# Attention, a ReLU MoE and a routed MoE on one core: the mask added by TensorE, global rows copied once, and the hand-over to the routed experts re-ordered

## The chip, the core and the metric

The kernel runs on one of the cores of a Trainium2 chip. Five engines each take their instructions in order: TensorE (PE; its weight loads are listed as PEld), VectorE (DVE), ScalarE (ACT), GpSimd (POOL) and SyncE (SP, which here issues most of the DMAs). They meet by semaphores only. The metric is the device time of one execution in microseconds, as a median of several runs; the profile is of one further execution.

## What is computed

```python
def reference(...):
    # 1. attention, 4 batches x 8 heads, 512 local + 32 global rows, head_dim 64
    out_g = softmax(scale * q_g @ [k_g, k_l]^T) @ [v_g, v_l]
    s_ll  = where(|i - j| <= 32, scale * q_l @ k_l^T, -1e9)
    out_l = softmax([scale * q_l @ k_g^T, s_ll]) @ [v_g, v_l]
    x = concat([out_g, out_l]) as 2176 tokens x 512
    # 2. MoE 1: two dense layers, 512 -> 2048 -> 512, leaky ReLU 0.01
    x = leaky(x @ w_in) @ w_out
    # 3. MoE 2: each token goes to one of 8 experts (argmax of cosine / tau)
    e = argmax(logits);  out = gate * (relu(x @ w1[e]) @ w2[e])   # 512 -> 1024 -> 512
```

The weights of MoE 1 arrive as 64-bit floats and are converted on the chip.

## The kernel before

**Three stages overlap.** The front (slots 0 to 20) does attention alone, while ACT, DVE and POOL convert w_in and w_out (`conv`: two ACT casts of the raw words, three DVE operations on bits, one ACT cast and one POOL subtraction for each of 32 pieces). Then the loop over `steps` runs MoE 1 (`L1`, `L2`) on PE with the rest of the attention between its matmuls. Last come 22 or more blocks of MoE 2, 128 tokens of one expert each.

**Attention.** `QK(n, 0)` and `QK(n, 1)` transpose the keys and queries of a pair of heads into `kT` and `qz`; `gnp` holds the transposed global rows, from which `kg` (global keys) and `gz` (global queries, padded with zeros so that one head stands in each half) are copied. `S(p)` multiplies, and DVE takes each 128x224 piece of scores, adds the mask, scales, writes it to SBUF and keeps the minimum (L211); ACT takes the exponential of it (L217); DVE divides (L223). `TR` transposes the probabilities, `AV` multiplies by the values. `GS`, `GT`, `GA` do the same for global rows. PSUM slots are shared by tag, two to a tag: `bank` says which tag a tile takes (S, H, Y or T), and a tile whose name isn't in it takes T.

**MoE 2.** Blocks alternate between two lanes: even blocks s use the expert weights in w1a and w2a, odd ones those in w1b and w2b (`load_w`, a conditional DMA that is skipped if the lane already holds that expert). Matmuls are done in three passes of fp32r, so the weights have to be split into a high and a low part: ACT casts 128x1024 (L849) and DVE subtracts (L850), 8 pieces a block. `M1(s, j)` is one half of the first layer, `HT(s, j)` transposes the hidden half (`tp`, then ACT cast and DVE subtraction `ht`), `M2(s, j)` is the second layer, `X2(s)` transposes the gathered tokens (`xgp`, `xgT`). The hidden half `hs` is cut at zero by ACT for j = 0 and by DVE for j = 1.

**The hand-over.** The last three token tiles leave MoE 1 only when blocks 0 and 1 could begin. Their routing is woven into the blocks by the table `due`: `Q1` (transpose `x2p` and logits `lp`), `Q2` (argmax, 11 small DVE operations), `Q3` (ranks `rp` and counts `cp` by matmul), `Q4` (positions, then three scatters of ids by POOL and six stores of rows by SP), `late_plan` (the plan for blocks 6 and later, 32 small DVE operations). `first` is the list of the weight pieces of block 0, which are split during the last steps of MoE 1. `half` is a pool of 8 buffers that holds first the weights of MoE 1 and then w1b, w2b and the split weights.

**What sets the order.** PE's order is that of the code everywhere. DVE's and SP's are that of the code in blocks 0 to 3. Elsewhere a scheduler orders DVE, ACT, POOL and SP when the kernel is built; an engine never overtakes within its order at run time.

Of the kernel before, what the change touches and what calls it, by code (L numbers as in the profile page):

```python
# [11 lines left out]
I32 = mybir.dt.int32  # L12
# [8 lines left out]
NEG = -8.0e9  # L21
# [3 lines left out]
def kernel(  # L25
# [114 lines left out]
    gzs = [att.tile([P, 2, SG], F32, name=f"gz{i}") for i in range(2)]  # L140
    for t in gzs:
        nc.vector.memset(t[D:P, 0], 0.0)
        nc.vector.memset(t[0:D, 1], 0.0)
# [7 lines left out]
    bank = {"sp0": "S", "sp1": "H", "sg1": "S"}  # L151
# [6 lines left out]
    def QK(n, j):  # L158
        qn, kn, gn = natural[n]
        if j == 1:  # L160
# [4 lines left out]
            nc.scalar.copy(qz, qv)  # L165
# [93 lines left out]
    def GS(n):  # L259
        sg1 = ps.tile([P, SL], F32, tag=bank_of("sg1"), name="sg1")  # L260
        sg2 = ps.tile([P, SG], F32, tag=bank_of("sg2"), name="sg2")
        for j in range(4):
            o = slice(SG * j, SG * j + SG)
            kT, gz = qkT[n - 1 + j // 2]
            lq = gz[:, j % 2, :]
            nc.tensor.matmul(sg1[o, :], lq, kT[:, :, 0:P], start=True, stop=True, tile_position=(0, SG * j))
            nc.tensor.matmul(
                sg2[o, :], lq, kT[:, NC - 1, P:P + SG], start=True, stop=True, tile_position=(0, SG * j)
            )
# [59 lines left out]
    def conv_load(i):  # L329
# [226 lines left out]
    def Q1(q):  # L556
# [36 lines left out]
    def Q3():  # L593

        ob = lt_["ob3"]
        rp = ps.tile([P, NL, E], F32, tag="T", name="rp")
# [7 lines left out]
        cp = ps.tile([1, E], F32, tag="T", name="cp")  # L604
# [121 lines left out]
    def make_plan(early):  # L726
# [33 lines left out]
        else:  # L760
            V.tensor_tensor(out=nb, in0=nb, in1=taken, op=ALU.subtract)
        V.tensor_tensor(out=pre, in0=lt, in1=nb.unsqueeze(1).to_broadcast([1, E, E]), op=ALU.mult)
# [4 lines left out]
        else:  # L767
# [9 lines left out]
            posf = pos.rearrange("o l i -> o (l i)")  # L777
        shp = [1, n, E]
# [8 lines left out]
        V.tensor_reduce(out=ex, in_=a2, axis=AX.X, op=ALU.add)  # L787
        if early:
# [18 lines left out]

        m = n // NLANE
# [80 lines left out]
    def M1(s, j):  # L889
# [9 lines left out]
        if j == 0:  # L899
# [311 lines left out]
```

## Time and profile before

| what | value |
|---|---|
| time, median of 3 runs (range) | 933.41 us (931.83 to 934.14) |
| the profiled execution, its own time | 931.04 us |
| its span, first to last instruction | 929.1 us |
| PE, PEld busy | 93 %, 78 % |
| DVE, ACT, POOL busy | 69 %, 60 %, 19 % |
| mean granted TensorE clock | 0.963 |

Busy shares are means over stages that have different limits, so the profile is read stage by stage: the table of stretches gives for each engine how much of a stretch it was busy, the timeline gives single instructions with the idle time ahead of them in brackets and what ended it, and the granted clock is 1.00 at 2.4 GHz and 0.50 at 1.2 GHz.

### The profile page before, as it was taken

Reading aid. Unit: us, or ns where it says so; the run is one execution under the profiler, and the core shown is the slowest. Engines: PE = TensorE matmul, PEld = TensorE weight load, DVE = VectorE, ACT = ScalarE, POOL = GpSimd, SP = SyncE. Lnnn points to the kernel's source line nnn. Section 1 sums busy time; section 2 is a strip of 40 time slices with the busy share of each in tenths; the row PEclk is TensorE's granted clock in tenths of the full one; section 3 lists DMA queues with packets and bytes.
Section 4 is the critical chain, followed back from the end, with each engine's and each line's share of the span. In section 5 each row is a group of like instructions: output and inputs, shape, how many; then the busy total and the mean of one; then the engine's idle time right before and its main releaser. Section 6 shows DMA issues by size and latency. Waiting matters only on the chain.

```text
span 929.1 us, 15882 instructions
## 1 busy us (share of the span) xinstructions
PE 863.6 (93%) x5578; PEld 727.1 (78%) x5578; DVE 639.2 (69%) x1557; ACT 561.6 (60%) x1206; POOL 173.5 (19%) x220
## 2 busy tenths in 40 slices
PE   3766799999999999999999999997899999999997
PEld 2555587888888888888888988986687888888885
DVE  6998888444664654554544435556989989999996
ACT  5877876544544644445433232364687888888885
POOL 3423433000210110010000000120233222231311
PEclk9776799999999999999999999997999999999999
DMA  8875562120122121110000000554315118829550
GB/s 215 197 215 149 146 189 69 33 45 17 29 61 44 25 57 29 44 30 3 13 12 1 24 1 24 193 187 73 24 58 215 35 46 328 276 78 384 191 202 26
DMA packets 104995, 92.68 MB, mean 100 GB/s; under 512 B 73735, under 2 KB 82055, under 8 KB 104914
## 3 DMA queue, kind: packets, MB, share of 16 engines
q1 hardware_dynamic: 97618, 77.47, 27.7%
q0 software_dynamic: 4224, 10.78, 4.2%
q10 hardware_dynamic: 3072, 3.41, 1.2%
q8 instruction: 45, 0.74, 0.4%
q14 instruction: 36, 0.29, 0.1%
HBM read 140.03 MB, written 11.63 MB: 163 GB/s over the span
## 4 chain that ended last, share of the span: by engine, by line
PE 73%; DVE 9%; issue 6%; DMA 6%; ACT 5%; POOL 1%; SPq 1%; POOLq 0%; ACTq 0%; DVEq 0%
PE hps L669 20%; PE hp L895 10%; PE yp L923 9%; PE yp L691 7%; PE yp L693 6%; PE yp L692 6%; PE av L247 3%; PE pp L233 2%; PE sp L199 2%; PE tp L909 2%; DMA qn<-in_q_l_dram 1%; DMA ids<-idl 1%; ACT pr L217 1%; PE lp L499 1%; DVE pr L223 1%
## 5 line engine op out<-in xcount | busy, mean ns | idle before, releaser
L676 ACT COPY gf<-hps 128x256 f32<-128x256 f32 (+1 forms) x144 | 50.2, 360 | 175.2 <-PE hps L669 168.4
L677 DVE SCALAR_TENSOR_TENSOR gf<-gf 128x256 f32<-128x256 f32 (+1 forms) x144 | 60.7, 429 | 129.3 <-ACT gf L676 127.7
L895 PE MATMUL hp<-w1s,xgT 128*128 128x512 f32 x528 | 139.1, 413 | 0.0
L923 PE MATMUL yp<-w2s,ht 128*128 128x512 f32 x528 | 130.9, 396 | 1.0 <-DVEq L1175 1.0
L923 PEld LDWEIGHTS yp<-w2s,ht 128*128 128x128 f32 x528 | 98.8, 188 | 25.7 <-DVEq L1175 1.4
L895 PEld LDWEIGHTS hp<-w1s,xgT 128*128 128x128 f32 x528 | 100.0, 196 | 21.4
L691 PE MATMUL yp<-woh,g 128*128 128x512 f32 x272 | 114.8, 422 | 0.0
L693 PE MATMUL yp<-woh,g 128*128 128x512 f32 x272 | 107.7, 396 | 0.0
L692 PE MATMUL yp<-wol,g 128*128 128x512 f32 x272 | 107.7, 396 | 0.0
L680 DVE TENSOR_TENSOR g<-gf,g 128x256 fp32r<-128x256 f32 (+1 forms) x144 | 57.7, 409 | 39.3 <-ACT g L679 35.0
L669 PE MATMUL hps<-xs,wih 128*128 128x256 f32 x448 | 75.7, 291 | 5.7 <-ACT gf L676 4.2
L679 ACT CAST g<-gf 128x256 fp32r<-128x256 f32 (+1 forms) x144 | 55.3, 395 | 36.1 <-DVE gf L677 36.1
L669 PEld LDWEIGHTS hps<-xs,wih 128*128 128x128 f32 x448 | 65.0, 189 | 12.5 <-ACT gf L676 4.9
L669 PE MATMUL hps<-xs,wil 128*128 128x256 f32 x448 | 71.3, 281 | 0.0
L669 PE MATMUL hps<-xl,wih 128*128 128x256 f32 x448 | 71.2, 280 | 0.0
L217 ACT ACTIVATE pr<-pr,nm 128x224 f32<-128x224 f32 x128 | 60.6, 475 | 2.7 <-DVE nm L211 1.8
L693 PEld LDWEIGHTS yp<-woh,g 128*128 128x128 f32 x272 | 51.2, 188 | 12.7 <-DVE g L680 0.2
L669 PEld LDWEIGHTS hps<-xs,wil 128*128 128x128 f32 x448 | 60.9, 189 | 0.0
L669 PEld LDWEIGHTS hps<-xl,wih 128*128 128x128 f32 x448 | 60.9, 189 | 0.0
L691 PEld LDWEIGHTS yp<-woh,g 128*128 128x128 f32 x272 | 51.3, 189 | 11.7 <-issue 4.5
L850 DVE TENSOR_TENSOR w2s<-w2a,w2s 128x1024 fp32r<-128x1024 f32 x48 | 56.7, 1218 | 2.8 <-ACT w2s L849 2.6
L850 DVE TENSOR_TENSOR w1s<-w1a,w1s 128x1024 fp32r<-128x1024 f32 x48 | 56.5, 1217 | 1.8 <-ACT w1s L849 1.7
(257 smaller groups left out, 1705.1 us busy)
## 6 DMA issues: line engine op xcount, KB each, us to landing
w1a<-in_moe_w_dram SPq DMA_DIRECT2D x12, 2048.0 KB
w2a<-in_moe_w_dram SPq DMA_DIRECT2D x12, 2048.0 KB
w1b<-in_moe_w_dram SPq DMA_DIRECT2D x12, 2048.0 KB
w2b<-in_moe_w_dram SPq DMA_DIRECT2D x12, 2048.0 KB
raw<-in_moe_w_in_dram SPq DMA_DIRECT2D x13, 512.0 KB
raw<-in_moe_w_out_dram SPq DMA_DIRECT2D x13, 512.0 KB
x2d<-x SPq DMA_DIRECT2D x16, 256.5 KB
kn<-in_k_l_dram SPq DMA_DIRECT2D x31, 128.0 KB
```

Of the source, the lines that this page charges most:

```text
L217: nc.scalar.activation(out=pr, in_=pr, func=AF.Exp, bias=nm[:, j:j + 1], scale=-1.0, accum_out=sm[:, j:j + 1],)
L669: nc.tensor.matmul(hps, ws[a][:, k], xs[c][k], start=(a + c + k == 0), stop=((a, c) == (1, 0) and k == KM - 1))
L676: nc.scalar.copy(gf, hps[:, cs])
L677: nc.vector.scalar_tensor_tensor(out=gf, in0=gf, scalar=0.01, in1=gf, op0=ALU.mult, op1=ALU.max)
L679: nc.scalar.copy(g[:, 0], gf)
L680: nc.vector.tensor_tensor(out=g[:, 1], in0=gf, in1=g[:, 0].bitcast(F32), op=ALU.subtract)
L691: nc.tensor.matmul(yp, g[:, 0], hi, start=(f == 0), stop=False)
L692: nc.tensor.matmul(yp, g[:, 0], lo, start=False, stop=False)
L693: nc.tensor.matmul(yp, g[:, 1], hi, start=False, stop=(f == KF - 1))
L850: nc.vector.tensor_tensor(out=w[:, 1, c], in0=src[:, c], in1=w[:, 0, c].bitcast(F32), op=ALU.subtract)
L895: nc.tensor.matmul(hp_, xT[:, a, k, :], w[:, c, k, :], start=(a + c + k == 0), stop=(c == 1 and k == KM - 1))
L923: nc.tensor.matmul(yp, ht[:, a, f, :], w[:, c, f, :], start=(j + a + c + f == 0), stop=(j == c == 1 and f == 3))
```

## The change

1. **Mask by PE in the front.** While the front's bank table is in force, a bf16 identity times the bf16 mask starts each score tile (one 128x448 matmul for each of the two heads), and the score matmuls add to it. DVE takes the maximum straight from PSUM, two reductions of 2x224 instead of four masked passes, and ACT's exponential reads PSUM instead of SBUF. The factor 0.125 goes into the copy of `qz`. After the front the old form stays.
2. **Global rows copied once.** `gz` holds keys and queries side by side, in one copy from `gnp` instead of three; `GS` uses the 64 partitions of each head instead of zero padding. The two border copies of `kT` go from DVE to ACT. In the front `kp` takes tag H and `gnp` takes tag S instead of T.
3. **First raw loads** of the conversion are issued by SP, behind the first q, instead of by ACT.
4. **Second lane loaded in MoE 1.** `load_w(1)` stands at step 10 of MoE 1's last round instead of behind it; `first` holds only the two halves of w1 of block 0, and its w2 follows behind the last step.
5. **Late routing.** Logits, ranks and counts share one tile on tag Y; logits become a step of their own (`Q1L`); Q2 to Q4 come later, and `late_plan` is cut in five pieces between places of blocks 1 and 2.
6. **`hs`** is cut at zero by ACT for both halves of blocks 0 to 4.

```diff
+    ALONE = dict(sp0="S", sp1="H", sg1="S", pp="Y", av="T", gp="Y", gq="T", ga="T", qp="T", kp="H", gnp="S")
-        nc.vector.tensor_copy(kT[:, 1:NC, 0:SG], kp[:, 0:NC - 1, P - SG:P])
-        nc.vector.tensor_copy(kT[:, 0:NC - 1, WIN - SG:WIN], kp[:, 1:NC, 0:SG])
+        nc.scalar.copy(kT[:, 1:NC, 0:SG], kp[:, 0:NC - 1, P - SG:P])
+        nc.scalar.copy(kT[:, 0:NC - 1, WIN - SG:WIN], kp[:, 1:NC, 0:SG])
...
-        nc.vector.tensor_copy(kg, gp[:, 0:SG])
-        for h in range(2):
-            r = slice(64 * h, 64 * h + 64)
-            nc.vector.tensor_copy(gz[r, h, :], gp[r, SG:2 * SG])
+        nc.vector.tensor_copy(gz.rearrange("p a s -> p (a s)"), gp)
...
+        for h in range(2 if pe_mask else 0):
+            nc.tensor.matmul(sps[h], identb, mask[:, kind(c0):kind(c0) + 2, :], start=True, stop=False)
...
+            if pe_mask:
+                nc.vector.tensor_reduce(
+                    out=nm[:, 2 * h:2 * h + 2], in_=sps[h], axis=AX.X, op=ALU.max, negate=True
+                )
+                continue
...
-            (nc.scalar if i < 6 else nc.sync).dma_start(t, src.bitcast(I32))
+            (nc.scalar if 2 <= i < 6 else nc.sync).dma_start(t, src.bitcast(I32))
...
+            rt["bank"] = ps.tile([P, 2 * NL + 1, E], F32, tag="Y", name="lr")
...
-        if j == 0:
+        if j == 0 or s < 5:
             nc.scalar.activation(out=hs, in_=hp_, func=AF.Relu)
...
+                load_w(1)
+                first = pieces_w1(0, 0) + pieces_w1(0, 1)
...
+    for piece in pieces_w2(0, 0) + pieces_w2(0, 1):
+        tc.keep_in_program_order(piece())
...
-        (0, "a"): [(Q1, (0,)), (Q1, (1,))], (0, "b"): [(Q1, (2,))], (0, "c"): [(Q2, ())],
-        (0, "d"): [(Q3, ())], (0, "e"): [(Q4, ())], (1, "a"): [(late_plan, ())],
+        (0, "a"): [(Q1, (0,)), (Q1, (1,))], (0, "b"): [(Q1L, (0,)), (Q1L, (1,)), (Q1, (2,))], (0, "d"): [(Q1L, (2,))],
+        (0, "e"): [(Q2, ())], (1, "a"): [(Q3, ())], (1, "c"): [(Q4, ())], (1, "e"): [(late_plan, ())],
+        (1, "f"): [(late_plan, ())], (2, "a"): [(late_plan, ())], (2, "d"): [(late_plan, ())], (2, "e"): [(late_plan, ())],
```

**Where instructions move.** On PE, at the hand-over, before: the first M1 of block 0 (`hp_7324`), the routing of the late tiles, the second M1 of block 0 (`hp_7362`), and the first M1 of block 1 (`hp_7500`) behind ranks and counts.

```order
L895 MATMUL hp_7324<-w1s,xgT 128x512 x12
L560 MATMUL x2p<-ident,x_7310 128x128 x4
L566 MATMUL lp<-enT,x2T 128x8 x4
L560 MATMUL x2p<-ident,x_7314 128x128 x4
L566 MATMUL lp<-enT,x2T 128x8 x4
L895 MATMUL hp_7362<-w1s,xgT 128x512 x12
L560 MATMUL x2p<-ident,x_7318 128x128 x4
L566 MATMUL lp<-enT,x2T 128x8 x4
L909 MATMUL tp<-ident,hs 128x128 x4
L881 MATMUL xgp<-ident,xg 128x128 x4
```

The same place on PE after the change; `lr` is the shared tile, `hp_7317` the second M1 of block 0, `hp_7435` the first M1 of block 1.

```order
L910 MATMUL hp_7288<-w1s,xgT 128x512 x12
L565 MATMUL x2p<-ident,x_7264 128x128 x4
L565 MATMUL x2p<-ident,x_7268 128x128 x4
L910 MATMUL hp_7317<-w1s,xgT 128x512 x12
L576 MATMUL lr<-enT,x2T 128x8 x8
L565 MATMUL x2p<-ident,x_7272 128x128 x4
L924 MATMUL tp<-ident,hs 128x128 x4
L896 MATMUL xgp<-ident,xg 128x128 x4
L576 MATMUL lr<-enT,x2T 128x8 x4
L924 MATMUL tp<-ident,hs 128x128 x4
L910 MATMUL hp_7435<-w1s,xgT 128x512 x12
```

The logits of the first two late tiles went behind the second M1 of block 0, and ranks and counts behind the first M1 of block 1.

On DVE at the same place, before, from the copies of the late tiles on: the hidden half of `hp_7362`, the argmax (first and last row of 11), then block 1's pieces of w1b.

```order
L562 COPY x2T<-x2p 128x512 x2
L902 TENSOR_SCALAR hs<-hp_7362 128x512
L562 COPY x2T<-x2p 128x512
L580 TENSOR_SCALAR sl_7304<-sl_7304,tau_sb 128x3
...
L590 TENSOR_TENSOR lg_7305<-lg_7305,sl_7304 128x24
L850 TENSOR_TENSOR w1s<-w1b,w1s 128x1024 x2
L912 TENSOR_TENSOR ht<-tp,ht 128x512
L884 TENSOR_TENSOR xgT<-xgp,xgT 128x512
```

DVE after the change, from the same copies to the same argmax.

```order
L567 COPY x2T<-x2p 128x512 x2
L865 TENSOR_TENSOR w2s<-w2a,w2s 128x1024 x3
L567 COPY x2T<-x2p 128x512
L865 TENSOR_TENSOR w2s<-w2a,w2s 128x1024
L865 TENSOR_TENSOR w1s<-w1b,w1s 128x1024 x2
L927 TENSOR_TENSOR ht<-tp,ht 128x512
L899 TENSOR_TENSOR xgT<-xgp,xgT 128x512
L590 TENSOR_SCALAR sl_7258<-sl_7258,tau_sb 128x3
```

Four pieces of w2a and two of w1b now stand ahead of the argmax, and the hidden half is gone from DVE.

On SP at the program's start after the change, the raw loads stand between the first q and the second pair's keys; before, ACT issued them, behind its own k and q.

```order
L88 DMA kn<-in_k_l_dram 128x4x64
L94 DMA gn<-in_k_g_dram 32x4x64
L94 DMA gn<-in_q_g_dram 32x4x64
L88 DMA qn<-in_q_l_dram 128x4x64
L345 DMA raw<-in_moe_w_in_dram 128x4x256
L345 DMA raw<-in_moe_w_out_dram 128x1024
```

Two loads of 512 KB moved from ACT's queue to SP's.

## Rows read from the trace of the kernel before

**Rows 1.** Busy time by stretch: PE, PEld, DVE, ACT, POOL us; PE clock, DMA share, GB/s.

```profile
0.00:106.00 106.00, 66.87 (x519) 50.48 (x520) 89.94 (x261) 80.10 (x205) 39.73 (x67) 0.79 0.74 194
...
150.00:616.00 466.00, 464.86 (x3387) 406.25 (x3383) 241.02 (x885) 210.29 (x619) 42.27 (x71) 1.00 0.14 37
616.00:725.00 109.00, 96.53 (x451) 78.29 (x450) 87.56 (x138) 73.91 (x99) 25.39 (x21) 0.92 0.42 114
```

**Rows 2.** Timeline of PE at the hand-over: start us, us, instruction [idle before <-releaser].

```profile
621.62 2.96 PE L895 MATMUL hp<-w1s,xgT 128*128 128x512 f32 x12
...
661.86 1.12 PE L909 MATMUL tp<-ident,hs 128*128 128x128 f32 x4 [3.83 <-DVE hs L902]
...
689.05 3.08 PE L895 MATMUL hp<-w1s,xgT 128*128 128x512 f32 x12
...
703.43 0.66 PE L909 MATMUL tp<-ident,hs 128*128 128x128 f32 x4 [2.02 <-DVE hs L902]
...
703.84 3.08 PE L895 MATMUL hp<-w1s,xgT 128*128 128x512 f32 x12
...
716.39 3.04 PE L895 MATMUL hp<-w1s,xgT 128*128 128x512 f32 x12
```

**Rows 3.** Timeline of ACT at the hand-over.

```profile
624.62 0.60 ACT L900 ACTIVATE hs<-hp 128x512 f32<-128x512 f32 x1 [0.67 <-PE hp L895]
...
630.55 1.99 ACT L849 CAST w2s<-w2b 128x1024 fp32r<-128x1024 f32 x2 [3.46 <-DMA w2b<-in_moe_w_dram]
```

**Rows 4.** Timeline of DVE at the hand-over.

```profile
635.12 0.69 DVE L902 TENSOR_SCALAR hs<-hp 128x512 f32<-128x512 f32 x1 [6.91 <-PE hp L895]
...
639.12 2.35 DVE L850 TENSOR_TENSOR w1s<-w1b,w1s 128x1024 fp32r<-128x1024 f32 x2
641.39 0.68 DVE L912 TENSOR_TENSOR ht<-tp,ht 128x512 fp32r<-128x512 f32 x1
641.99 0.68 DVE L884 TENSOR_TENSOR xgT<-xgp,xgT 128x512 fp32r<-128x512 f32 x1
642.58 0.17 DVE L612 TENSOR_TENSOR sr<-rp,base_e 128x24 f32<-128x24 f32 x1
...
643.91 2.34 DVE L850 TENSOR_TENSOR w2s<-w2b,w2s 128x1024 fp32r<-128x1024 f32 x2
...
651.31 0.15 DVE L741 TENSOR_SCALAR wk<-cp 1x8 f32<-1x8 f32 x1
...
657.67 2.34 DVE L850 TENSOR_TENSOR w1s<-w1a,w1s 128x1024 fp32r<-128x1024 f32 x2
```

**Rows 5.** The chain that ended last, in order of time, 0 to 12 us.

```profile
2.35 8.25 DMA qn<-in_q_l_dram
```

**Rows 6.** Timeline of DVE in the first 14 us.

```profile
5.93 0.26 DVE L177 COPY kT<-kp 128x96 f32<-128x96 f32 x1 [1.18 <-ACT kT L176]
6.11 0.25 DVE L178 COPY kT<-kp 128x96 f32<-128x96 f32 x1
6.27 0.18 DVE L181 COPY kg<-gnp 128x32 f32<-128x32 f32 x1
6.37 0.38 DVE L184 COPY gz<-gnp 64x32 f32<-64x32 f32 x2
10.25 0.69 DVE L365 SCALAR_TENSOR_TENSOR t<-t,t 128x512 int32<-128x512 int32 x1 [3.50 <-ACT t L359]
```

**Rows 7.** Timeline of DVE around a score tile, 26 to 34 us.

```profile
26.86 0.66 DVE L271 TENSOR_REDUCE gm<-sg 128x1 f32<-128x512 f32 x1
27.43 0.18 DVE L272 TENSOR_REDUCE gm<-sg 128x1 f32<-128x32 f32 x1
...
30.66 0.38 DVE L211 CUSTOM_DVE_ANT_0 pr<-sp,mask 128x224 f32<-128x224 f32 x1
...
30.97 0.38 DVE L211 CUSTOM_DVE_ANT_0 pr<-sp,mask 128x224 f32<-128x224 f32 x1
```

**Rows 8.** Groups in 0 to 106 us: line, form, count | busy us, mean ns | idle before.

```profile
L217 ACT ACTIVATE pr<-pr,nm 128x224 f32<-128x224 f32 x43 | 20.3, 474 | 1.8 <-DVE nm L211 1.8
```

More of the change, by code (lines that the diff above doesn't have):

```diff
@@ L139 @@
     qz = att.tile([P, NC * P], F32, name="qz")
[L140 to L143, printed above, removed]
+    identb = att.tile([P, P], BF16, name="identb")
+    nc.vector.tensor_copy(identb, ident)
     ves = [att.tile([P, NC + 1, 2, D], F32, name=f"ve{i}") for i in range(2)]
@@ L164, in QK @@
             qv = qp.rearrange("k c p -> k (c p)")
-            nc.scalar.copy(qz, qv)
+            nc.scalar.activation(out=qz, in_=qv, func=AF.Copy, scale=0.125)
             natural.pop(n)
@@ L199, in S @@
                 nc.tensor.matmul(
-                    sps[h][:, i, :], qz[r, c * P:(c + 1) * P], kT[r, c, :], start=True, stop=True,
-                    tile_position=(D * h, 0),
+                    sps[h][:, i, :], qz[r, c * P:(c + 1) * P], kT[r, c, :],
+                    start=not pe_mask, stop=not pe_mask or i == 1, tile_position=(D * h, 0),
                 )
@@ L264, in GS @@
             kT, gz = qkT[n - 1 + j // 2]
[L265 to L269, printed above, removed]
+            r = slice(D * (j % 2), D * (j % 2) + D)
+            at = (D * (j % 2), SG * j)
+            nc.tensor.matmul(sg1[o, :], gz[r, 1], kT[r, :, 0:P], start=True, stop=True, tile_position=at)
+            nc.tensor.matmul(sg2[o, :], gz[r, 1], kT[r, NC - 1, P:P + SG], start=True, stop=True, tile_position=at)
         gm = att.tile([P, 4], F32, tag="gm", bufs=2, name="gm")
@@ L595, in Q3 @@
         ob = lt_["ob3"]
-        rp = ps.tile([P, NL, E], F32, tag="T", name="rp")
+        rp = rt["bank"][:, NL:2 * NL]
         nc.tensor.matmul(rp, tri, ob[:, 0:NL], start=True, stop=False)
@@ L603, in Q3 @@
                 nc.tensor.matmul(rp[:, q, :], ones, ob[:, o, :], start=False, stop=(q == NL - 1 and o == q - 1))
[L604 removed]
+        cp = rt["bank"][0:1, 2 * NL, :]
         for q in range(NL + 1):
@@ L1051 @@
             plan_constants()
-            make_plan(True)
+            for _ in make_plan(True):
+                pass
             load_w(0)
@@ L1088 @@
             if k == KF * (2 * B - 1) + 10:
-                first = pieces_w1(0, 0) + pieces_w1(0, 1) + pieces_w2(0, 0) + pieces_w2(0, 1)
-            for piece in first[:2 if len(first) > 6 else 1]:
+                lanes[1] = (
+                    sb.tile([P, KM, F2], F32, tag="half", bufs=8, name="w1b"),
+                    sb.tile([P, KF2, DM], F32, tag="half", bufs=8, name="w2b"),
+                )
+                load_w(1)
+                first = pieces_w1(0, 0) + pieces_w1(0, 1)
+            for piece in first[:1]:
                 tc.keep_in_program_order(piece())
-            first = first[2 if len(first) > 6 else 1:]
+            first = first[1:]
         if slot == LAST and not hold and att is not None:
@@ L1102 @@
         k += 1
-    lanes[1] = (
-        sb.tile([P, KM, F2], F32, tag="half", bufs=8, name="w1b"),
-        sb.tile([P, KF2, DM], F32, tag="half", bufs=8, name="w2b"),
-    )
-    for piece in first:
-        piece()
-    load_w(1)
     load_w(2)
@@ L1115 @@
             Q0(t, ys.pop((2 * B - 1, t)))
+    for piece in pieces_w2(0, 0) + pieces_w2(0, 1):
+        tc.keep_in_program_order(piece())
+    plan_pieces = make_plan(False)
     def late_plan():
-        make_plan(False)
-        for q in range(NEARLY, NEARLY + 3):
-            load_ids(q)
+        if next(plan_pieces, "done") == "done":
+            for q in range(NEARLY, NEARLY + 3):
+                load_ids(q)
     def block(s, end, begin=0):
```

37 lines of the change are left out of this document (22 added, 15 removed).

## The prediction

> **What bounds the kernel now.** I read the table of stretches first, then the timelines of PE, ACT and DVE in the two stretches where PE isn't full, and the chain of waits at the program's start. The table splits the span in three. From 150 to 616 us PE is busy 464.86 of 466 us at full clock [rows 1]: nothing that the change does to DVE, ACT or SP there can shorten it, and PE's instructions there stay what they are. From 0 to 106 us (attention alone) PE is busy 66.87 us only, while DVE has 89.94 and ACT 80.10 of 106 [rows 1]: two engines near their limit that hand work to each other, which the chain of waits crosses by turns. From 616 to 725 us PE loses 12.5 of 109 us, at a mean clock of 0.92, with DVE at 87.56 [rows 1]. After that PE is full again, one block in 716.39 - 703.84 = 12.55 us [rows 2]. So there are two places to gain, the front and the hand-over, and a microsecond gained in either goes through to the end, because behind both PE is the bound with the same work.
>
> In the hand-over the reader is to see a late start of DVE. It sits idle for 6.91 us before 635.12 [rows 4], because ACT waits 3.46 us for the second lane's w2 at 630.55 [rows 3], and because the second M1 of block 0 stands on PE behind two logits that wait for copies. From 639.12 on DVE is never idle, and it is late: PE waits 3.83 us at 661.86 and 2.02 us at 703.43 for an `hs` that stands in DVE's queue behind splits and behind the late plan (651.31 to 657.67, 6.36 us) [rows 2, 4].
>
> **The hand-over, step by step.** Common zero is the first M1 of block 0 at 621.62 [rows 2]; PE is full before it in both kernels, and in the new one DVE and ACT have less to do before it (block 0's w2 is no longer split there).
>
> *Where DVE starts.* ACT ends block 0's first `hs` at 624.62 + 0.60 = 625.2 [rows 3]; then, by the new order, come four casts of w2a, 1.99 for two [rows 3], so the first is there at 626.2. The two copies x2T are done by then (their transposes follow M1 at once).
>
> *What DVE must do until the tokens of block 4 are split (xgT of block 4, the last thing that M1 of block 4 needs).* From rows 4, by the distance between starts: a pair of weight pieces 641.39 - 639.12 = 2.27; ht 0.60; xgT 0.59; Q4 643.91 - 642.58 = 1.33; the plan 6.36; the argmax at most 639.12 - 635.12 less hs and a copy (0.6 each) = 2.8, its wait for logits included. In the new order there stand, up to that xgT: 4 pieces of w2 of block 0, 8 each of blocks 1 to 3, 2 of block 4, together 30, or 15 pairs = 34.05; 7 ht = 4.2; 4 xgT = 2.4; one copy of a late tile 0.6; argmax 2.8; Q4 1.33; the whole plan 6.36. The four `hs` of blocks 0 to 3 (0.6 each) are gone to ACT. Sum 51.7. One wait must be added: ACT's exponential of the late logits stands in its queue ahead of w2b's casts and waits for the argmax, so the next cast (1.0) begins only then: 1.3 with the exponential. 626.2 + 51.7 + 1.3 = 679.2.
>
> *What PE makes of it.* Until there PE has eight M1, six M2 (2.96 at most at full clock) and some 5 us of transposes and logits, about 47 us from 621.62, or 669: less than DVE needs, so DVE is the bound and M1 of block 4 starts at 679.2 instead of 689.05 [rows 2]. From there one block is 12.55, so M1 of block 5 starts at 691.8 instead of 703.84, since the second wait of 2.02 for `hs` also goes. **Gain 12 us.** Edits that I cost at nothing: ACT gains five `hs` (0.6 each), but its casts take 1.0 where DVE's subtractions take 1.13, so DVE's time covers them; the shared tile keeps one of two Y slots until the plan's first piece, before M2 of block 1 wants it; the three scatters and the ids of block 6 start with Q4, which comes some 4 us later than at 642.58 [rows 4], but are wanted by block 5's transposes, at about 697; the loads of the second lane, 4 MB, run in a stretch whose DMA share is 0.14 [rows 1]. On SP, that load now stands ahead of the first lane's next load and the late rows' stores behind the third block's load; none of these is waited for in the walk above. Were the cover gone (DVE not the bound), the gain would be larger by PE's 10 us of slack; if ACT were, smaller, see the rivals. Bounds: 9 (each of four blocks loses 0.75 us to waits that I don't see) to 13.
>
> **The front, step by step.** *The start.* The first q load of SP takes 8.25 us [rows 5], and stands on the chain; two raw loads of 512 KB were issued by ACT beside it. In the new order they stand on SP behind q, so q shares the DMA engines with small loads alone. The queries then come some 4 us sooner, and the copy qz stands ahead of the first conversion on ACT. DVE's idle time of 3.50 before 10.25 [rows 6] can be filled, and the pair behind it is loaded sooner as well. Bounds 0 to 6; I take 4, near the row of the idle time.
>
> *DVE's work.* Eleven S in the front. Masked passes start 0.31 apart, four to an S, 1.24; a reduction of 128x512 takes 27.43 - 26.86 = 0.57 [rows 7], so 2x224 costs an estimated 0.50 by its columns, 1.00 for two: 11 x 0.24 = 2.6. Six QK: two border copies 0.18 + 0.16 = 2.0; three copies of global rows 0.10 + 0.38 against one of 0.18 = 1.8 [rows 6]. DVE loses 6.4 of its 89.94. *ACT's work.* It gets twelve border copies; no row shows one on ACT, so I price them by DVE's own, 0.25 [rows 6]: 3.0 on top of 80.10, which brings both engines to some 83. The end of the front follows now the one, now the other: between 6.4 gained and 3.0 lost; I take 2 gained, near the mean of both. The mask matmuls (22, on an engine that is idle 39 of 106 us [rows 1], placed ahead of qz's arrival) and the moves of kp and gnp to other tags I cost at 0. **Gain 6 us**, bounds -3 to 12.4.
>
> A rule of the Trainium skill speaks against the first step. What the row shows is one load of 128 KB that takes 8.25 us while raw loads run [rows 5]. The Trainium skill, DMA: Bandwidth & Descriptors, section "Issuing engines are not separate DMA queues", says that transfers run on the same 16 DMA engines and interleave whichever engine issued them, so that another issuer saves only issue time. By that rule the start gains nothing, which is rival A; no run here shows it yet.
>
> **The sum.** The profiled execution took 931.04 us, its span 929.1 and 1.9 us around it, 2.4 us below the median of 933.41. 931.04 - 12 - 6 = 913; at the median 933.41 - 18 = **915.4 us**.
>
> **Rivals.** A: q shares the DMA engines with the raw loads wherever they are issued, their place in SP's queue changes nothing, and the front gains 2 only: 933.4 - 14 = 919.4. For it: DMA is busy 0.74 of the front [rows 1], so transfers may simply move the wait. Against it: q and the raw loads came from two queues, and now stand in one, q first. B: DVE alone is the front's bound and all of it is gained: 933.4 - 12 - 12.4 = 909. For it DVE's 89.94 against ACT's 80.10 [rows 1]; against it ACT's new 83. C: ACT becomes the bound of the hand-over, as the hidden halves stand behind up to six casts there, and PE waits for them as it did for DVE, say 1.5 us in each of four blocks: 933.4 - 6 - 6 = 921.4. For it the wait on the exponential; against it 1.0 to 1.13 a piece. D, on the other side: score tiles now stay in PSUM until ACT has taken four exponentials, 4 x 0.474 = 1.9 us [rows 8], where DVE's passes freed them before, and with gnp and kp in the same tags the next S may have to wait that long. If all eleven S stand on the chain with it: 11 x 1.9 = 21, 933.4 - 18 + 21 = 936. It decides from 1.6 us an S. Against it: an S comes every 106 / 11 = 9.6 us. E: the second lane's load doesn't start in MoE 1, since its buffer isn't free. In the new order its w1 is first cast behind four other casts and a hidden half, its w2 behind the argmax, so even then it would cost 1 to 3 us: inside the forecast's range.
>
> **How the numbers follow.** Forecast with E (910 to 918.5) 0.54, A 0.21, B 0.09, C 0.10, D 0.04, others 0.02. The predicted time is the forecast's, 915. The range takes in B below with a better hand-over (933.4 - 13 - 12.4 = 908) and above A with the hand-over at 9 or C with a front of 3 (922.4 to 924.4): 907 to 925. What a measurement of this kernel can tell from no change is 0.3 %, about 2.8 us: only C with a lost front or a part of D lies between 930.6 and 936. Faster 0.93, same 0.03, slower 0.04.
>
> **What would show it.** Right: the first scores matmul at about 8 us instead of 13, L1 of MoE 1 some 6 us sooner; no wait for `hs` at the hand-over, M1 of block 1 about 14 us behind that of block 0, M1 of block 5 at 70 us behind it instead of 82.2; DVE without a gap over 2 us from 626 on (by the common zero). Wrong: PE waits for ACT's `hs`, a DVE that waits for ACT's casts, waits of the mask matmul for an exponential, or a q load that still takes 8 us. The forecast fails if the scheduler's new order of ACT or DVE puts a long wait ahead of work that PE needs, which the order alone doesn't tell.

## The result, and the profile after

The changed kernel takes 920.15 us (median of 4 runs, 915.88 to 921.67), the kernel before 932.82 in the same session: a ratio of 0.9858, 95% interval 0.9825 to 0.9892. The gain is 12.7 us; 18 were forecast, and the time stands 5 us above the forecast's 915, inside its range. The profiled execution took 921.5 us with a span of 919.7.

The table of stretches, after, answers to [rows 1]; one stretch is added, 96 to 156 us, where MoE 1 runs between the matmuls of the attention while the last of its weights are converted (the recorded expectations call MoE 1 "MoE 0"). Columns: busy us (count) of PE, PEld, DVE, ACT, POOL, then PE's granted clock, DMA share, GB/s.

```profile
0.00:106.00 106.00, 75.77 (x544) 51.80 (x545) 84.66 (x171) 82.02 (x226) 42.17 (x68) 0.79 0.72 189
96.00:156.00 60.00, 50.18 (x359) 41.95 (x355) 52.97 (x110) 45.93 (x115) 26.03 (x21) 0.89 0.50 140
150.00:616.00 466.00, 463.65 (x3373) 405.00 (x3372) 232.80 (x841) 208.32 (x627) 42.00 (x71) 1.00 0.16 46
616.00:725.00 109.00, 100.84 (x488) 81.38 (x487) 95.05 (x144) 86.12 (x117) 45.43 (x24) 0.97 0.28 79
```

In the hand-over PE gained 4.3 us of work and DVE 7.5. In the front PE is 8.9 us busier, but the second row shows it neither full nor at full clock in the 60 us behind it. The same stretch before:

```profile
96.00:156.00 60.00, 52.99 (x415) 43.86 (x412) 54.55 (x138) 46.07 (x118) 23.67 (x21) 0.92 0.50 138
```

So PE does less there than before. It starts with more done and ends 1 us ahead.

**The hand-over.** The timeline of PE, after, answers to [rows 2] (start us, us, instruction, idle before and its releaser in brackets): the first M1 of blocks 0, 4, 5 and 6, then the transposes and the second M1 of block 6.

```profile
620.57 2.96 PE L910 MATMUL hp<-w1s,xgT 128*128 128x512 f32 x12
...
677.97 3.32 PE L910 MATMUL hp<-w1s,xgT 128*128 128x512 f32 x12
...
690.76 3.04 PE L910 MATMUL hp<-w1s,xgT 128*128 128x512 f32 x12
...
703.26 3.04 PE L910 MATMUL hp<-w1s,xgT 128*128 128x512 f32 x12
711.08 0.66 PE L924 MATMUL tp<-ident,hs 128*128 128x128 f32 x4 [1.97 <-ACT hs L915]
711.92 4.58 PE L910 MATMUL hp<-w1s,xgT 128*128 128x512 f32 x12
```

The first M1 of block 5 stands 690.76 - 620.57 = 70.2 us behind that of block 0, instead of 82.2. Behind it something new: the second M1 of block 6 starts 8.66 us after the first, where 6.5 is usual, and takes 4.58 instead of 3.04. ACT's timeline shows where the `hs` was that PE waited for at 711:

```profile
707.47 0.69 ACT L945 ACTIVATE yo<-yp,gate 128x512 f32<-128x512 f32 x1 [5.16 <-DMA out_dram<-yo,ids]
...
710.42 0.60 ACT L915 ACTIVATE hs<-hp 128x512 f32<-128x512 f32 x1
```

ACT stood 5.16 us at a `yo` whose buffer still waited to be scattered; `hs` was queued behind it. POOL's timeline shows why the scatter was late:

```profile
673.10 5.68 POOL L946 DMA_INDIRECT out_dram<-yo,ids  x1 [6.80 <-DMA out_dram<-yo,ids]
679.09 3.21 POOL L854 DMA_INDIRECT xg<-x2d,ids  x1 [0.31 <-issue]
682.61 7.07 POOL L854 DMA_INDIRECT xg<-x2d,ids  x1 [0.31 <-issue]
689.98 7.70 POOL L854 DMA_INDIRECT xg<-x2d,ids  x1 [0.30 <-issue]
697.99 2.60 POOL L946 DMA_INDIRECT out_dram<-yo,ids  x1 [0.30 <-ACT ht L926]
```

Five indirect DMAs in a row take 2.6 to 7.7 us each to issue; 1.0 to 2.0 is usual (1.00 at 708.19).

**The front.** PE's timeline at its end: the first L1 starts at 96.50 instead of 104.06, and the two instructions behind it wait 3.45 and 2.73 us.

```profile
96.50 0.72 PE L680 MATMUL hps<-xs,wih 128*128 128x256 f32 x4
...
101.61 1.12 PE L239 MATMUL pp<-ident,pr 128*128 128x128 f32 x4 [3.45 <-ACT pr L223]
105.46 1.22 PE L680 MATMUL hps<-xs,wih 128*128 128x256 f32 x4 [2.73 <-ACT gf L687]
```

PE idles most of 98 to 105, and its granted clock falls to the lower level (1.2 GHz, a granted 0.50) in the next stretch, so that the four matmuls of an L1, 0.72 us at 96.50, take 1.22 at 105.46:

```profile
95.00:100.00 5.00, 3.16 (x34) 2.72 (x32) 4.89 (x10) 3.48 (x11) 1.51 (x1) 1.00 0.55 138
100.00:105.00 5.00, 1.12 (x4) 0.72 (x4) 4.66 (x7) 3.89 (x11) 3.52 (x3) 0.64 0.25 93
105.00:110.00 5.00, 4.54 (x18) 4.06 (x19) 4.60 (x10) 2.97 (x9) 1.07 (x2) 0.50 0.67 188
```

From the first L1 to the first M1 of block 0 the changed kernel takes 524.1 us, the kernel before 517.6. That is where the lead of 7.6 us went: the first M1 of block 0 starts at 620.57 instead of 621.62.

### The profile page after: what moved, and what is told of

It reads as the page before. It is cut to its first block, busy times and chain, and to the rows that moved or that the text cites. A ratio compares the mean times of both kernels' runs of the same rounds, so it can differ in the third digit from the quotient of the medians.

```text
span 919.7 us, 15811 instructions
## 1 busy us (share of the span) xinstructions
PE 869.8 (95%) x5600; PEld 726.0 (79%) x5600; DVE 623.5 (68%) x1419; ACT 566.3 (62%) x1243; POOL 191.1 (21%) x220
## 4 chain that ended last, share of the span: by engine, by line
PE 72%; DMA 8%; issue 6%; DVE 5%; ACT 5%; POOL 2%; SPq 0%; POOLq 0%; ACTq 0%; DVEq 0%
PE hps L680 21%; PE hp L910 8%; PE yp L702 7%; PE yp L938 7%; PE yp L704 7%; PE yp L703 6%; PE av L253 3%; PE pp L239 3%; PE sp L202 2%; DMA out_dram<-yo,ids 2%; POOL xg L854 2%; DMA ids<-idl 1%; ACT pr L223 1%; PE ga L314 1%; PE lp L504 1%
## 5 line engine op out<-in xcount | busy, mean ns | idle before, releaser
L910 PEld LDWEIGHTS hp<-w1s,xgT 128*128 128x128 f32 x528 | 98.1, 193 | 24.9 <-DVE xgT L899 4.4
L691 DVE TENSOR_TENSOR g<-gf,g 128x256 fp32r<-128x256 f32 (+1 forms) x144 | 60.7, 431 | 42.9 <-ACT g L690 39.9
L946 POOL DMA_INDIRECT out_dram<-yo,ids x22 | 33.8, 1537 | 143.6 <-ACT yo L945 129.7
L854 POOL DMA_INDIRECT xg<-x2d,ids x24 | 48.2, 2010 | 60.9 <-PE hps L680 21.6
```

The costliest lines, as they stand in the source:

```text
L691: nc.vector.tensor_tensor(out=g[:, 1], in0=gf, in1=g[:, 0].bitcast(F32), op=ALU.subtract)
L854: nc.gpsimd.indirect_dma_start(out=xg, out_offset=None, in_=x2d[:, :], in_offset=bass.IndirectOffsetOnAxis(ap=ids[:, s:s + 1].bitcast(U32) ...
L910: nc.tensor.matmul(hp_, xT[:, a, k, :], w[:, c, k, :], start=(a + c + k == 0), stop=(c == 1 and k == KM - 1))
```

## The experiments

All times are medians; the ratio is to the kernel before on the same chip. The last columns are read from the one profiled execution of each kernel: the start of block 0's first M1, and how far behind it block 5's stands. Executions of the changed kernel lie 5.8 us apart, so a difference of 2 us in these columns decides nothing alone; the changed kernel, e7 and e8, which are the same up to there, start block 0 at 619.55 to 621.27.

| kernel | us | ratio (95%) | M1 of block 0 | block 5 behind |
|---|---|---|---|---|
| before | 932.82 | 1 | 621.62 | 82.2 |
| changed | 920.15 | 0.9858 (0.9825-0.9892) | 620.57 | 70.2 |
| e1 front only | 929.75 | 0.9984 (0.9970-0.9998) | 616.81 | 82.6 |
| e2 hand-over only | 921.40 | 0.9894 (0.9876-0.9911) | 621.35 | 70.2 |
| e3 raw loads on SP only | 936.20 | 1.0050 (1.0031-1.0068) | 627.01 | 80.5 |
| e5 changed, raw loads on ACT again | 920.98 | 0.9872 (0.9850-0.9894) | 621.92 | 69.4 |
| e6 changed, nearly all raw loads on ACT | 924.09 | 0.9904 (0.9883-0.9925) | 624.15 | 71.9 |
| e7 changed, four yo buffers | 918.31 | 0.9849 (0.9831-0.9868) | 619.55 | 70.7 |
| e8 changed, hs on DVE again | 929.16 | 0.9958 (0.9943-0.9973) | 621.27 | 79.8 |
| e11 changed, subtraction on DVE | 912.90 | 0.9801 (0.9780-0.9822) | 613.61 | 70.2 |
| e12 hand-over only, subtraction on DVE | 919.19 | 0.9845 (0.9823-0.9867) | 619.56 | 71.4 |
| e4, e9, e10 (work left out) | - | - | 619.30, 618.45, 617.02 | - |

**e1 and e2, the two halves alone.** e1 is the kernel before with items 1 to 3 of the change, e2 with items 4 to 6. One more part of the change goes with e2: the split pieces of blocks 0 and 1 are kept in the order of the code.

> The kernel before with the front's parts of the change alone (mask by PE, one copy of global rows, first raw loads on SP). Theory 'the front's gain is given back in MoE 0': the first L1 of MoE 0 starts some 7 us sooner (97 instead of 104), but from 155 us on PE is no more than 1 to 1.5 us ahead of the kernel before, because the conversion of the MoE weights ends at 154 to 156 us as before; first M1 of block 0 at 620 to 621, time 1 us below before (932). Rival 'a microsecond gained in the front goes through': first M1 of block 0 at 615 to 616, time 6 us below (927).

> The kernel before with the hand-over's parts alone (second lane loaded in MoE 1, late routing in pieces and on one tile, hs on ACT). Theory 'nearly all of the gain is the hand-over's, less a loss behind it': the first M1 of block 5 stands 70 to 71 us behind that of block 0 instead of 82.2 (12 us gained), indirect DMAs of POOL take 3 to 8 us each between 670 and 700, a yo waits about 5 us for a buffer near 705 and 2 to 4 us of the 12 are lost there: time 8 to 10 us below before (923 to 925). Rival 'the loss near 710 comes from the front's part': no yo wait, time 12 us below (921). Rival 'the hand-over needs the front's part': under 6 us below.

The front's parts are worth 1.7 us at the medians (931.43 to 929.75): nearly nothing of their lead reaches the end. In the profiled execution of e1 4.8 us did, between the bounds of both theories, but it was the shortest of twelve (926.47).

The hand-over's parts are worth 10.0; 921.40 is below their theory's 923 to 925. Their profiled execution, again the shortest (918.53), shows the forecast's 12 at block 5 (82.2 - 70.2) and no long wait behind it: ACT waits 1.5 us for a `yo` buffer, and the steps of M1 stay at 6.5, although POOL's indirect DMAs there take up to 7.74 us. That looks like the rival "the loss comes from the front's part", but the other traces speak against it: e12, without the front's parts, waits 6.0 us for a `yo` buffer, and e6 and e10, with them, not at all. Among the kernels with this hand-over the wait is 4.8 to 6.0 us in four (changed, e5, e11, e12), 1.5 and 1.9 in e2 and e4, and none in e6 and e10. So it comes in some executions only.

**e3, e5 and e6, the raw loads.**

e3 makes this edit on the kernel before; e5 undoes it in the changed kernel:

```diff
-            (nc.scalar if i < 6 else nc.sync).dma_start(t, src.bitcast(I32))
+            (nc.scalar if 2 <= i < 6 else nc.sync).dma_start(t, src.bitcast(I32))
```

e6, on the changed kernel:

```diff
-            (nc.scalar if 2 <= i < 6 else nc.sync).dma_start(t, src.bitcast(I32))
+            (nc.scalar if i >= 2 else nc.sync).dma_start(t, src.bitcast(I32))
```

> The kernel before with one edit: the first two raw loads are issued by SP behind the first q. Theory 'q was held up by the raw loads': the first q load lands some 3 to 5 us sooner and the first scores matmul starts at 8 to 10 us instead of 13.3; the time stays within 1 us of before, since MoE 0 gives it back. Rival A 'the issuing engine does not matter': q still takes about 8 us and scores start at 13. Rival 'the start goes through': time 4 us below.

> The changed kernel with one edit undone: the first two raw loads are issued by ACT again. Theory 'the first raw loads on SP cost in MoE 0 more than they give at the start' (alone they cost 4.8 us, since the queue on SP comes out in another order and raw loads 11 and 12 leave at 60 instead of 51 and 55): first scores at 11 to 13 us instead of 7.5, raw loads 11 and 12 issued by 56, conversions end at 152 or sooner, time 2 to 4 us below the changed kernel (916 to 918). Rival 'the early start is the whole of the front's gain': first M1 of block 0 at 622 to 625, time 2 to 4 us above it (922 to 924). Rival 'neither reaches the end': within 1 us of 920.

> The changed kernel with all raw loads but the first two issued by ACT instead of SP. ACT frees a raw buffer itself, so it issues the next load at once, and no raw load stands behind the loads of values and keys that wait on SP for PE. Theory 'SP's queue holds the conversion up': raw loads 11 and 12 leave at 50 to 56 instead of 60, the waits for raw data on ACT between 120 and 150 go, PE is full from 150 or sooner, time 2 to 5 us below the changed kernel (915 to 918). Rival 'ACT's time is the limit': 26 issues of 0.37 us are 9.6 us more on ACT in the first 155 us, the conversion ends later than 156, time 2 to 6 us above (922 to 926).

e3 does at the start what was expected. PE's timeline of e3 at the first scores:

```profile
7.91 1.86 PE L199 MATMUL sp<-kT,qz 64*128 64x224 f32 x8 [0.72 <-issue]
```

And the kernel before:

```profile
13.34 1.86 PE L199 MATMUL sp<-kT,qz 64*128 64x224 f32 x8 [1.51 <-ACT qz L165]
```

One edit, 5.4 us earlier; and the kernel is 4.8 us slower, which no theory had. The edit gives SP's queue another order. SP's timeline of the kernel before, at raw loads 11 and 12:

```profile
51.48 0.35 SPq L340 DMA_DIRECT2D raw<-in_moe_w_out_dram  x1
54.73 0.38 SPq L340 DMA_DIRECT2D raw<-in_moe_w_in_dram  x1
```

The same loads in e3 leave 9 and 6 us later, behind value loads (`vb`) whose buffers wait for PE:

```profile
59.58 0.43 SPq L119 DMA_DIRECT2D vb<-in_v_l_dram  x1
60.10 0.37 SPq L340 DMA_DIRECT2D raw<-in_moe_w_out_dram  x1
60.57 0.39 SPq L340 DMA_DIRECT2D raw<-in_moe_w_in_dram  x1
```

That this order is the cause is argued, not shown: e6 took the raw loads off SP, and the conversion did end 5 us sooner (150.9 instead of 156.2), but its first L1 came at 105.7 and the time rose. That is the rival's time, without the late conversion that the rival had for its cause. e5 shows the item's worth in the changed kernel: without it the first scores start at 11.79 instead of 7.47, the conversion ends at 152.3, and the time is the same, as its third theory had it.

**e4, no raw loads, and e9, no DVE passes, in the second half of the conversion.**

e4, in `conv_load` (`kept` holds the raw tiles of pieces 14 and 15):

```diff
+            if i >= 16:
+                raws[i] = kept[i % 2]
+                return
```

e9, in `conv_bits`, ahead of the three passes:

```diff
+        if i >= 16:
+            temps[i] = t
+            return
```

> The changed kernel, but the raw loads of conversion pieces 16 to 31 are left out: pieces 14 and 15 are converted again in their place, with the same instructions on ACT, DVE and POOL, so the MoE weights are wrong and the routing with them; only what stands ahead of the first M1 of block 0 is compared. Theory 'the two raw buffers bound the stretch from 96 to 155 us' (a load can't be issued before the buffer is read, and takes 4 to 5.5 us): without the loads the conversion ends at 140 to 148 instead of 156, PE is full from there, and the first M1 of block 0 stands 3 to 6 us sooner, at 615 to 617. Rival 'ACT's and DVE's own work bounds it': the conversion ends within 2 us of 156 and the first M1 of block 0 stays within 1 us of 620.6.

> The changed kernel with DVE's three passes of the conversion left out for pieces 16 to 31 (their ACT and POOL work stays), so the MoE weights and the routing are wrong; only what stands ahead of the first M1 of block 0 is compared. Some 28 to 35 us of DVE's work between 65 and 156 us are gone. Theory 'DVE's queue (90 per cent busy from 96 to 156) takes the front's gain back': PE's waits of 3.45 us at 101.6 and 2.73 at 105.5 fall below 1 us each, PE is full from 145 or sooner, first M1 of block 0 at 612 to 617. Rival 'ACT's queue is the limit': the waits stay above 2 us, first M1 of block 0 at 619 to 621.

Neither brings the lead back. In e4 the conversion ends at 154.8, M1 stands at 619.30: the two buffers don't bound the conversion. In e9 half of DVE's work in the stretch is gone (table of stretches, columns as above):

```profile
96.00:156.00 60.00, 51.86 (x388) 44.32 (x389) 26.96 (x70) 46.26 (x118) 21.24 (x20) 0.91 0.51 145
```

PE's timeline of e9 at the first and the second L1 shows the same two waits, little shorter or longer:

```profile
105.06 0.66 PE L239 MATMUL pp<-ident,pr 128*128 128x128 f32 x4 [2.39 <-ACT pr L223]
109.00 1.22 PE L683 MATMUL hps<-xs,wih 128*128 128x256 f32 x4 [3.28 <-ACT gf L690]
```

So DVE's passes don't make these two waits, and M1 at 618.45 misses the theory's 612 to 617 (and the rival's 619 to 621). But one sign of the theory came: PE is full from 140 on in e9, first row, and not in the changed kernel, second row.

```profile
140.00:156.00 16.00, 16.00 (x119) 14.06 (x118) 7.53 (x23) 8.11 (x24) 0.44 (x2) 1.00 0.27 61
140.00:156.00 16.00, 15.33 (x102) 12.54 (x101) 15.59 (x33) 12.96 (x33) 7.73 (x7) 0.93 0.48 127
```

And both runs reach their first L1 late, at 101.57 (e4) and 101.06 (e9) instead of 96.50. From there to block 0's M1 they take 517.7 and 517.4 us instead of 524.1. So the loss behind the first L1 is gone in them and another has come ahead of it; why is open, and the two runs don't settle what bounds the stretch.

For the two waits the chain of one piece from engine to engine remains, which is argued here, not shown. The changed kernel's timelines show it there. POOL:

```profile
100.21 1.39 POOL L382 TENSOR_TENSOR wil<-t,wih 128x512 fp32r<-128x512 f32 x1 [3.66 <-ACT wih L381]
101.56 1.27 POOL L288 TENSOR_TENSOR pg<-pg,gm 128x544 f32<-128x544 f32 x1
```

DVE beside it:

```profile
97.66 0.43 DVE L373 TENSOR_SCALAR t<-t 128x512 int32<-128x512 int32 x1
...
98.54 0.68 DVE L374 CUSTOM_DVE_ANT_0 t<-t,t 128x1024 uint16<-128x1024 uint16 x1
...
100.58 1.30 DVE L373 TENSOR_SCALAR t<-t 128x512 int32<-128x512 int32 x1
101.92 1.46 DVE L374 CUSTOM_DVE_ANT_0 t<-t,t 128x1024 uint16<-128x1024 uint16 x1
```

The same two passes take 0.43 and 0.68 us at 97.66 and 98.54, then 1.30 beside POOL's subtraction (L382) and 1.46 beside its multiplication of global probabilities (L288). ACT's next cast waits 1.11 us for the second, and the `gf` that PE waits for at 105.46 is queued behind that cast. Only the 1.30 belongs to the subtraction: e11 below, where the multiplication stays on POOL, has the 1.46 again.

```profile
101.80 0.43 DVE L373 TENSOR_SCALAR t<-t 128x512 int32<-128x512 int32 x1
102.26 1.46 DVE L374 CUSTOM_DVE_ANT_0 t<-t,t 128x1024 uint16<-128x1024 uint16 x1
```

**e10, e11 and e12, POOL's subtraction.**

e11, on the changed kernel, and e12, on the kernel of e2:

```diff
-            nc.gpsimd.tensor_tensor(out=lo, in0=src, in1=hi.bitcast(F32), op=ALU.subtract)
+            nc.vector.tensor_tensor(out=lo, in0=src, in1=hi.bitcast(F32), op=ALU.subtract)
```

e10 puts `nc.gpsimd.memset(lo.bitcast(F32), 0.0)` in that line's place for `i >= 16`.

> The changed kernel with POOL's subtraction of conversion pieces 16 to 31 replaced by a fill with zero, so the low halves of these MoE weights and with them the routing are wrong; only what stands ahead of the first M1 of block 0 is compared. Theory 'POOL's subtractions hold DVE up' (DVE's pass of 0.42 us takes 1.18 in the mean where a POOL subtraction runs beside it, 0.69 becomes 0.95): DVE's passes of pieces 16 to 31 take 0.42, 0.69 and 0.69 each, DVE is some 5 us less busy from 96 to 156, first M1 of block 0 at 615 to 618. Rival 'the longer passes are hidden': first M1 within 1.5 us of 620.

> The changed kernel with the conversion's subtraction on DVE instead of POOL, for all 32 pieces. DVE gets 32 x 0.69 = 22 us more, and loses the hold-ups beside POOL's subtractions, some 15 to 20 us up to 156 us. Theory 'POOL's subtraction costs DVE about what its own pass would': DVE's busy time from 0 to 156 stays within 6 us of 128, the chain of one piece gets shorter, time 2 below to 2 above the changed kernel (918 to 922). Rival 'each further pass on DVE counts in full': first M1 of block 0 10 us later or more, time above 928.

> The hand-over's parts alone, as in e2_hand (921.4), with the conversion's subtraction on DVE as in e11_subdve (912.9, which is the whole change with it); the two differ in the front's parts only. Theory 'POOL's subtractions took the front's gain': without them the front's parts are worth 5 to 8 us, so this kernel takes 918 to 921 and its first M1 of block 0 stands at 619 to 621.5. Rival 'POOL's subtractions cost every version alike': this kernel gains 6 to 8 as well, 913 to 916, first M1 of block 0 at 613.5 to 616, and the front's parts stay worth 1 to 3.

In e10 M1 lands in its theory's bounds (617.02), and DVE is 8.5 us less busy from 96 to 156 (44.52 instead of 52.97; some 5 were expected), but PE's two waits stay, 3.57 and 2.61 us. e11 is the best kernel of all: 7.3 us below the changed one by the medians, 5.3 by the ratios, 2 per cent below before, and better than its theory's 918 to 922. Its first M1 of block 0 stands 7 us earlier. Groups of DVE from 0 to 156 us in the changed kernel (line, form, count, busy us, mean ns, idle before):

```profile
L370 DVE SCALAR_TENSOR_TENSOR t<-t,t 128x512 int32<-128x512 int32 x32 | 25.0, 785 | 11.5 <-ACT t L364 6.3 <-ACT t L363 5.0
L373 DVE TENSOR_SCALAR t<-t 128x512 int32<-128x512 int32 x32 | 17.8, 563 | 0.9
```

The same groups in e11, and the two that are new there:

```profile
L370 DVE SCALAR_TENSOR_TENSOR t<-t,t 128x512 int32<-128x512 int32 x32 | 21.8, 685 | 11.6 <-ACT t L364 6.8 <-ACT t L363 4.6
L373 DVE TENSOR_SCALAR t<-t 128x512 int32<-128x512 int32 x32 | 13.3, 418 | 0.1
L382 DVE TENSOR_TENSOR wil<-t,wih 128x512 fp32r<-128x512 f32 x16 | 10.9, 684 | 0.0
L382 DVE TENSOR_TENSOR wol<-t,woh 128x512 fp32r<-128x512 f32 x16 | 10.9, 681 | 0.3 <-ACT woh L381 0.3
```

DVE takes on 21.8 us of subtractions and gets most of it back: it is busy 130.15 us up to 156 instead of 128.25. A subtraction takes 0.68 us there, on POOL some 1.5 in the mean. PE's wait at the second L1 falls from 2.73 to 0.93, the one ahead of it stays (3.80), and from the first L1, at 97.91, to block 0's M1 it takes 515.7 us instead of 524.1. Two things changed at once: DVE is no longer held up, and the subtraction itself, a step of the chain, is shorter. No run parts them.

The Trainium skill, SBUF — State Buffer, section "Who interferes with whom", says that DVE and GpSimd share a port pair, that an instruction of DVE with two SBUF inputs contends with a GpSimd one that reads SBUF, that one in a 2-port mode contends with GpSimd as well, and that the one behind then blocks wholly. The trace agrees that passes beside POOL's work take longer, by the 1.30 and 1.46 above; no view here shows the mode of a pass.

e12 was meant to tell whether this took the front's gain in particular. Its time and its M1 fall in that theory's bounds; but by ratios the move is worth 0.0049 without the front's parts (e2 to e12) and 0.0057 with them, and the front's parts 0.0036 without the move and 0.0044 with it, from ratios that are each uncertain by 0.002 to 0.003. So POOL's subtraction costs every version some 5 us, and whether it takes more from the front's gain stays open.

**e7, more buffers for yo, and e8, hs on DVE again.**

e7:

```diff
-        yo = sb.tile([P, DM], F32, tag="x2", bufs=2, name="yo")
+        yo = (late["pool"].tile([P, DM], F32, tag="xw", bufs=2, name="yo") if s % 2 else
+              sb.tile([P, DM], F32, tag="x2", bufs=2, name="yo"))
```

e8:

```diff
-        if j == 0 or s < 5:
+        if j == 0:
```

> The changed kernel with two more buffers for yo (odd blocks take a tag of their own). The order of instructions on PE, ACT, DVE and SP is the same. Theory 'ACT's wait for a yo buffer near 705, behind POOL's long indirect DMAs, is the loss of 3.7 us behind block 5': no wait of ACT for out_dram between 640 and 725, M1 of block 6 both 6.5 us or less apart, while POOL's indirect DMAs still take 3 to 8 us each at 673 to 700; time 2 to 4 us below the changed kernel where that wait occurs, 1 to 2 us below at the median. Rival 'the loss has another cause (hs on ACT behind casts)': steps of 8 us behind block 5 stay, time within 1 us.

> The changed kernel with the second hs of blocks 0 to 4 on DVE again. Theory 'DVE is the bound of the hand-over': five hs of 0.67 us go back on DVE, so M1 of block 5 stands 72.5 to 74 us behind that of block 0 instead of 70.2, time 2 to 3.5 us above the changed kernel. Rival 'the hs on ACT costs PE's wait what DVE gains': M1 of block 5 at 70 to 71 behind, time within 1 us. Rival 'POOL is held up by DVE's unbroken row of subtractions and a hs that reads PSUM lets it in': the long indirect DMAs shrink below 4 us, and the time is equal or lower.

In e7 ACT has no wait for `out_dram`, and the first M1 of block 6 and the second stand at 702.78 and 709.25. But the theory's condition didn't come: from 679 to 695 POOL's indirect DMAs take only 1.0 to 2.0 us each, and e6 and e10, with mostly short ones too and with the old two buffers, have no such wait either. So the changed kernel's trace shows that ACT waited for a buffer, and e7 doesn't show that more buffers take the wait away. By the medians e7 is 1.8 us faster, but the intervals overlap, so its worth is not settled.

e8 is the surprise: 9 us slower than the changed kernel, not 2 to 3.5. PE's timeline of e8 at block 3:

```profile
670.70 1.12 PE L924 MATMUL tp<-ident,hs 128*128 128x128 f32 x4 [4.44 <-DVE hs L917]
671.47 5.09 PE L910 MATMUL hp<-w1s,xgT 128*128 128x512 f32 x12
```

DVE's timeline one block later:

```profile
683.11 0.68 DVE L917 TENSOR_SCALAR hs<-hp 128x512 f32<-128x512 f32 x1
683.71 2.36 DVE L865 TENSOR_TENSOR w2s<-w2a,w2s 128x1024 fp32r<-128x1024 f32 x2
689.01 0.69 DVE L927 TENSOR_TENSOR ht<-tp,ht 128x512 fp32r<-128x512 f32 x1 [2.93 <-ACT ht L926]
```

PE waits 4.44 us for an `hs` in DVE's queue, and its M1 behind that runs near the lower clock (granted 0.55 from 671.5 to 676.5; 5.09 us for what takes 3.04). Later DVE itself stands 2.93 us, since the `ht` that it needs comes by way of PE and ACT. Each engine waits for the other by turns, and the 0.67 us of the `hs` itself is the smallest part of it. The third theory's sign came, without its gain: from 662 on POOL's indirect DMAs take 1.0 to 2.0 us.

## Why the prediction was right or wrong

- **Hand-over, 12 us: right where it was worked out, short behind it.** DVE's first piece of w2a starts at 625.28 (the sum, moved to this execution's zero, gives 625.2); M1 of block 4 starts at 677.97 and its xgT ends at 679.0, where the sum gives 678.2 for both. From 638 to 702 DVE waits 1.9 us in all, so it is the bound there as said. Block 5 came 70.2 behind block 0 (forecast 70). At the end e2 shows 10.0 by medians. The missing 2 fit the wait for a `yo` buffer, which some executions have and others don't; that they are the same is not shown.
- **One term of it was mis-sized.** The step counted the four `hs` as 0.6 each of DVE's time plus the wait of 2.02. e8 measures 9.6 of the 12 for them (79.8 against 70.2); the rest of the hand-over's parts give the other 2.4 as long as the `hs` are on DVE. No run has the `hs` on ACT without the rest. The misreading is in "from 639.12 on DVE is never idle": in the kernel before, DVE waits 4.6 us in three times for ACT's `ht` between 638 and 702. The longest:

```profile
679.28 0.69 DVE L912 TENSOR_TENSOR ht<-tp,ht 128x512 fp32r<-128x512 f32 x1 [2.94 <-ACT ht L911]
```

  That is the loop of e8. A sum of one engine's durations can't show it; the total came out right since it was worked out for the new order, where with `hs` on ACT the loop is gone and DVE is the bound.
- **Costed at nothing, and not nothing:** POOL's scatters and gathers. The step asked when their results are wanted, not how long POOL needs to issue them, nor who holds a buffer meanwhile. The signs "PE waits for ACT's `hs`" and no gap over 2 us on DVE both failed at 705 to 711 (DVE's gap is 3.12 us).
- **Front, the work: right in the main.** In 0 to 106 us, the stretch of the sum, DVE is busy 84.66 instead of 89.94, 5.3 less (forecast 6.4). Up to 156 us it is 6.4, but there eight pairs of heads were transposed and not six, so that match is luck. ACT's twelve border copies took 0.26 us each, 3.1 in all (forecast 3.0). The first scores start at 7.47 (forecast 8), L1 7.6 us sooner (forecast 6).
- **Front, the time: wrong.** The step that failed is "a microsecond gained in either goes through to the end, because behind both PE is the bound". It read 0 to 106 and 150 to 616 us and skipped what lies between, where PE is busy 52.99 of 60 us before and 50.18 after. Of 6 us, e1 measures 1.7 for the front's parts alone; on top of the hand-over's they are worth 0.9894 - 0.9858 = 0.0036, some 3 us, uncertain by 0.004. 10.0 and 1.7 to 3.3 add up to 11.7 to 13.3, which holds the 12.7. What in that stretch takes the lead is open: moving POOL's subtraction shortens it in e11, but e12 gains nearly as much from that without the front's parts.
- **Rival A** named nearly the measured time (919.4), for the wrong reason. Its rule, of the Trainium skill, DMA: Bandwidth & Descriptors, section "Issuing engines are not separate DMA queues", would, as the prediction applied it, leave q as late as it was; e3 has the scores 5.4 us earlier by that edit alone. That the edit gains nothing at the end is right (e5), but for the stretch behind the front.
- **Rival D** is there in small: the mask matmuls wait 6.9 us in four times for ACT's exponentials, in the front, where the lead is lost anyway. C came in small: PE waited for ACT's `hs` once early (3.1 us, near 643), against the sign "no wait for `hs`", and once behind the `yo`; the early one is covered, as block 4 came when the sum said. E didn't come: the loads of w1b and w2b were issued at 595.85 and 598.48 instead of 616.46 and 617.17. One sum was wrong: C with a front that gains nothing is 933.4 - 6 = 927.4, and 930.4 at the front's lower bound, so it doesn't lie above 930.6.

## What to carry to other kernels

Before a gain in one stage is booked, look at the stage right behind it, not only at the long one where an engine is full: a lead is kept only if nothing in between is bound by other engines. Where two engines hand work to each other, take an instruction that one of them waits for out of the longer queue; that is worth the loop, not the instruction. Work on POOL beside a busy DVE isn't free: here the same subtraction on DVE cost DVE 2 us more in all and saved the kernel 5 to 7.

## What the runs showed of the hardware

- DVE's passes of the conversion took longer beside elementwise work on POOL: 1.30 instead of 0.43 us beside a subtraction of 128x512 (1.39 us), 1.46 instead of 0.68 beside a multiplication of 128x544 (1.27 us).
- Indirect DMAs on POOL take 1.0 to 2.0 us to issue, and 5.68, 7.07 and 7.70 in the changed kernel, where DVE subtracts without a gap from 671 to 700 us, up to six times in a row with two operands in SBUF. Each ended within 1 us of the start of DVE's next subtraction from PSUM (677.84, 688.72, 696.73):

```profile
686.45 2.34 DVE L865 TENSOR_TENSOR w1s<-w1b,w1s 128x1024 fp32r<-128x1024 f32 x2
688.72 0.67 DVE L927 TENSOR_TENSOR ht<-tp,ht 128x512 fp32r<-128x512 f32 x1
```

  But such a row is not enough. In e7 an indirect DMA takes 2.01 us in the middle of the same row:

```profile
683.61 2.35 DVE L865 TENSOR_TENSOR w2s<-w2a,w2s 128x1024 fp32r<-128x1024 f32 x2
684.87 2.01 POOL L947 DMA_INDIRECT out_dram<-yo,ids  x1 [0.30 <-ACT ht L926]
```

  The traces part by something else. In e6, e7, e8 and e10 DVE once stood 1.0 us or more for ACT's `ht` between 677 and 687, and at least the next three indirect DMAs took 1.0 to 2.0 us each. In the changed kernel, e2, e4, e5, e11 and e12 DVE didn't stand between 668 and 700, and in each two or three of them took 6.7 to 7.7. Why is open; no run took the subtractions away there.
- A wait of 6 us in 7 on PE cost more than itself: the granted clock stood at 0.50 in the 5 us behind it, and four matmuls of an L1 took 1.22 us there instead of 0.72.
